# Two attentions on one core: B's memory update built as three-head bands in four 32-column quarters of the TensorE array, all five tiles in one PSUM bank

## The chip, the core and the metric

The kernel runs on one core of a Trainium2 chip. The core's engines run side by side, each through its own instruction stream in order: TensorE (PE, with its weight loads shown apart as PEld), VectorE (DVE), ScalarE (ACT), GpSimd (POOL) and SyncE (SP, which issues most transfers). They wait for one another through semaphores. The metric is the device time of one execution in microseconds, as the median of several runs; lower is better. A profile shows one execution, with the time of every instruction.

## What is computed

Two attention layers over 2048 positions with 32 heads of 18 columns each: A shares one key and value head among all query heads; B works in four segments of 512 positions and carries a memory from one segment to the next. The output is both results side by side. The change touches only the memory of B, whose part of the reference is this:

```python
phi = lambda t: jnp.where(t > 0, t + 1.0, jnp.exp(t))
for s in range(N):                       # N = 4 segments of L = 512
    qs, ks, vs = q[:, :, s], k[:, :, s], v[:, :, s]
    ...
    pq = phi(qs)
    num = jnp.einsum("bhld,bhde->bhle", pq, M)
    den = jnp.einsum("bhld,bhd->bhl", pq, z)[..., None] + 1e-6
    a_mem = num / den
    o = g * a_mem + (1.0 - g) * a_dot
    pk = phi(ks)
    M = M + jnp.einsum("bhld,bhle->bhde", pk, vs)    # per head 18 x 18
    z = z + jnp.einsum("bhld->bhd", pk)
```

## The kernel before

The program has two phases. The first (to line 606) makes the projections of A and then, in a loop over the four segments `s` of B, the projections of B, the stores of queries, keys and values to DRAM, and the memory. The second (from line 675) is the attention itself, whose order on PE, ACT and DVE is written out by hand; it begins after a branch on a flag that the first phase computes (line 609). The order of the first phase is set by a scheduler, from the order in which the code is written and its own costs; some instructions are pinned to program order (`pin`).

The 32 heads lie in five tiles of seven, seven, seven, seven and four heads (`HT`), so a tile has `RT` = 126 or 72 rows, 18 for each head; `H0` is a tile's first head. For each segment but the last, the keys after `phi` are transposed so that positions lie on partitions (`natural`, line 415, writes `pkN` with four blocks `i` of 128 positions). The values lie in `vch` in the same layout, with a column of ones ahead of each head's 18 values, so a head takes `VW` = 19 columns; the ones give `z`.

The update of the memory stands at the end of a segment's turn of the loop (lines 576 to 601). For each tile `t`, four matmuls over the four blocks of positions take all the tile's keys (126 columns of weights) times the values of all its heads (7 x 19 = 133 columns): a product of every key column with every head's values, of which only each head's own block is wanted. VectorE multiplies the product with a mask (`bmask`) that leaves the blocks on the diagonal, adds it into `Mbd`, copies the values' part to `Mst` and sums the column of ones into `zc` and from there into `zst`. The product of a tile goes to the PSUM tile `mm`, of which there is one buffer, so the next tile's matmuls wait until VectorE has read the one before. `Mst` and `zst` are the weights with which later queries read the memory: of segments 0 and 1 they are stored to DRAM (`mzB`, lines 600 and 601) and read back in the second phase, of segment 2 they are used in the first phase (lines 432 and 548).

Lines that the prediction names: 252 is a projection matmul (128 rows, 126 columns, 512 positions); 494 a projection of values; 418 a transposition of the keys after `phi`; 557 are the matmuls of the bound of the scores (32 columns of weights each, put side by side in the array); 582 the memory's matmuls; 591 to 598 its VectorE steps; 450, 122 and 391 what VectorE does with a projected key tile; 208, 214 and 216 the split of the next inputs on VectorE; 243 a split of weights on POOL; 381, 382 and 481 POOL's zeroing of `Mst`, `zst` and the ones of `vch`; 778 (output projection of the second phase) and 973 (probabilities times values) are the other matmuls of 32 columns of weights in four quarters.

An fp32 matmul shows in the profile as two records of PE (and two weight loads): line 582 has 5 x 4 matmuls in each of three segments and 120 records.

Of the kernel before, what the change touches and what calls it, by code (L numbers as in the profile page):

```python
# [8 lines left out]
F32 = mybir.dt.float32  # L9
# [5 lines left out]
ALU = mybir.AluOpType  # L15
AX = mybir.AxisListType
# [6 lines left out]
C = 512  # L23
NCH = S // C
NKT = S // 128
HT = [7, 7, 7, 7, 4]
RT = [18 * h for h in HT]
H0 = [0, 7, 14, 21, 28]
SCALE = DH ** -0.5
BOUND_UP = 1.0 + 2.0 ** -6  # L30

# [4 lines left out]
VW = DH + 1  # L36
# [38 lines left out]
def attention_pair_kernel(ctx, tc, a_xT, a_w, a_wo, b_xT, b_w, b_wo, b_beta, ident_d, hmask_d, bmask_d, cmask_d, sel_d, zmask_d, selx_d, sely_d, out):  # L75
    nc = tc.nc
# [79 lines left out]
    with ExitStack() as ph:  # L156
# [3 lines left out]
        ps = ph.enter_context(tc.tile_pool(name="ps", bufs=1, space=PSUM))  # L160
# [13 lines left out]
        bmask = pw.tile([128, 7, VW], F32, name="bmask")  # L174
        zmask = pw.tile([128, 5, 32], F32, name="zmask")
# [87 lines left out]
        for c in range(NCH):  # L263
            ready = {}
            if c == 0:
# [11 lines left out]
                for k in range(5):  # L277
# [3 lines left out]
                    for i, (w, x) in enumerate(parts_):  # L281
                        for t in TILES:
# [5 lines left out]
                                start=k == 0 and i == 0,  # L288
                                stop=k == 4 and i == 1,
# [8 lines left out]
            for t in TILES:  # L298
# [3 lines left out]
                else:  # L302

                    nm, bufs = ("nd", 2) if c == 1 and t == 4 else ("pj", 4)
                    pj = ps.tile([128, C], F32, name=nm, bufs=bufs)
                    proj(pj[:M], wAh, wAl, xh, xl, 126 * t, M)
                R = RT[t]
# [22 lines left out]
                i = 5 * (c - 2) + TILES.index(t)  # L330
# [31 lines left out]
        for t in range(5):  # L362
            R = RT[t]
# [11 lines left out]


        p2 = ph.enter_context(tc.tile_pool(name="p2", bufs=1))
        Mbd = p2.tile([128, 5, 7, VW], F32, name="Mbd")
        Mst = p2.tile([128, 5, 7, DH], F32, name="Mst")
        zst = p2.tile([128, 5, 32], F32, name="zst")  # L380
        nc.gpsimd.memset(Mst, 0.0)
        nc.gpsimd.memset(zst, 0.0)
        zc = p2.tile([128, 5], F32, name="zc")
# [21 lines left out]
        for s in range(NSEG):  # L405
# [6 lines left out]
            pkN = p2.tile([128, 5, 4, 126], F32, name="pkN")  # L412
# [67 lines left out]
            vch = p2.tile([128, 4, H, VW], F32, name="vch")  # L480
# [86 lines left out]
            with tc.issue_after(sent.ins):  # L567
# [5 lines left out]
                if s == 2:  # L573
                    load_q(st0, qA[0], 0)
                    load_shift(st0, shA[0], slice(0, 8))
            if s < NSEG - 1:
                for t in range(5):
                    R = RT[t]
                    nh = HT[t]
                    pm = ps.tile([128, C], F32, name="mm", bufs=1)  # L580
                    for i in range(4):
                        nc.tensor.matmul(
                            pm[:R, : nh * VW],
                            pkN[:, t, i, :R],
                            vch[:, i, H0[t] : H0[t] + nh, :].rearrange("p h d -> p (h d)"),
                            start=i == 0,
                            stop=i == 3,
                        )
                    pmv = pm[:R, : nh * VW].rearrange("p (h d) -> p h d", d=VW)
                    if s == 0:  # L590
                        nc.vector.tensor_tensor(Mbd[:R, t, :nh], pmv, bmask[:R, :nh], op=ALU.mult)
                    else:
                        mx = p2.tile([128, 7, VW], F32, name="mx", bufs=1)
                        nc.vector.tensor_tensor(mx[:R, :nh], pmv, bmask[:R, :nh], op=ALU.mult)
                        nc.vector.tensor_tensor(Mbd[:R, t, :nh], Mbd[:R, t, :nh], mx[:R, :nh], op=ALU.add)
                    nc.vector.tensor_copy(Mst[:R, t, :nh], Mbd[:R, t, :nh, 1:VW])
                    nc.vector.tensor_reduce(zc[:R, t : t + 1], Mbd[:R, t, :nh, 0], axis=AX.X, op=ALU.add)
                    nc.vector.tensor_scalar(zst[:R, t], zmask[:R, t], zc[:R, t : t + 1], None, op0=ALU.mult)
                if s + 1 in LATE_ASK:
                    nc.sync.dma_start(mzB[:, s, :, :126], Mst.rearrange("p t h d -> p t (h d)"))  # L600
                    nc.sync.dma_start(mzB[:, s, :, 126:], zst)
# [680 lines left out]
```

## Time and profile before

| what | value |
|---|---|
| median of three runs | 1412.04 us (1411.96 to 1413.07) |
| the profiled execution's own time | 1411.4 us |
| its span, first to last instruction | 1409.4 us |
| mean granted TensorE clock | 0.998 of full speed |
| PE busy | 1390.8 us, 99% of the span |
| DVE busy | 1047.8 us, 74% |
| ACT busy | 1198.2 us, 85% |
| first phase | from 0 to about 291 us |
| memory updates | 124.6 to 138.3 us, 177.8 to 191.1 us, 230.7 to 243.3 us |

Times are read from the start of the span. A row of the timeline gives the start, the time from the first start to the last end, the engine, line, operation, output and input, partitions x elements, and how many records were merged. PE's matmuls overlap: the time that a row of matmuls takes from the engine is the start of the next row less its own start, not its duration. A row of the windows gives the busy time of each engine in a stretch.

### The profile page before, as it was taken

To read this page: it belongs to the slowest core of one execution; us is meant where nothing else is said; L and a number is where in the kernel's file an instruction comes from. 1 tells how busy PE (TensorE), PEld (TensorE's weight loads), DVE (VectorE), ACT (ScalarE), POOL (GpSimd) and SP (SyncE) were. 2 spreads that over 40 slices of the span, in tenths; PEclk is the share of its full clock that TensorE was granted. 3 is DMA by queue.
4 is the path that set the end of the run, shared out by engine and by line. 5 is a ranking of instruction groups with operands and counts; after the bars stand their busy time and mean duration, and the time that the engine had idled before them with its cause. 6 is when DMAs were issued, how large, how long until landed. Compare 5 with 4: busy or idle time off the path is not lost.

```text
span 1409.4 us, 40568 instructions
## 1 busy us (share of the span) xinstructions
PE 1390.8 (99%) x17132; PEld 844.2 (60%) x17132; DVE 1047.8 (74%) x1567; ACT 1198.2 (85%) x1479; POOL 231.3 (16%) x326
## 2 busy tenths in 40 slices
PE   9999999989999999999999999999999999999998
PEld 6788888745544555555555555555555555555558
DVE  6656456477787778777878878776879778887873
ACT  4543434479999999999999999999999999999991
POOL 2431000003302310402110122113010220001002
PEclk9999999999999999999999999999999999999999
DMA  9866547467575445332312442333103321120012
GB/s 284 265 208 189 165 138 228 165 174 204 173 214 167 117 140 172 99 119 85 111 58 70 147 143 60 95 107 90 51 35 97 105 75 46 33 64 18 18 65 107
DMA packets 90724, 172.67 MB, mean 123 GB/s; under 512 B 14576, under 2 KB 22889, under 8 KB 90110
## 3 DMA queue, kind: packets, MB, share of 16 engines
q1 hardware_dynamic: 84122, 160.01, 36.7%
q0 software_dynamic: 1664, 4.78, 1.4%
q10 hardware_dynamic: 4752, 5.24, 1.1%
q8 instruction: 136, 2.23, 0.7%
q14 instruction: 50, 0.41, 0.1%
HBM read 99.32 MB, written 70.67 MB: 121 GB/s over the span
## 4 chain that ended last, share of the span: by engine, by line
PE 70%; ACT 4%; DVE 2%; issue 1%; DMA 1%; SPq 0%; POOL 0%; ACTq 0%; DVEq 0%
PE O L973 32%; PE E L925 20%; PE F L778 11%; ACT P L943 4%; PE E L933 3%; PE E L1183 2%; DVE W L940 1%; PE F L834 1%; DMA vseg<-vB 0%; DVE sm L729 0%; DMA woA<-a_wo 0%; PE F L1183 0%; PE O L1183 0%; DMA oA<-oe 0%; DVE oe L982 0%
## 5 line engine op out<-in xcount | busy, mean ns | idle before, releaser
L943 ACT ACTIVATE P<-E 128x1024 f32<-128x1024 f32 (+1 forms) x800 | 786.7, 1073 | 2.8 <-PE E L925 2.5
L940 DVE COPY W<-E 128x1024 f32<-128x1024 f32 (+2 forms) x416 | 453.8, 1091 | 142.4 <-PE E L925 81.2
L973 PE MATMUL O<-P,VA 128*32 128x256 f32 x7504 | 507.8, 380 | 0.0
L943 ACT ACTIVATE P<-W 128x1024 f32<-128x1024 f32 (+1 forms) x330 | 369.5, 1120 | 8.6 <-DVE W L940 7.9
L973 PEld LDWEIGHTS O<-P,VA 128*32 128x32 f32 x7504 | 259.7, 110 | 138.3 <-issue 6.2
L925 PE MATMUL E<-stA,kstA 56*128 56x512 f32 x1920 | 317.7, 430 | 3.9 <-DVE W L940 2.9
L925 PEld LDWEIGHTS E<-stA,kstA 56*128 56x128 f32 x1920 | 154.9, 185 | 161.4 <-issue 92.5
L948 POOL TENSOR_SCALAR_AFFINE_SELECT P<-P 128x256 f32<-128x256 f32 (+1 forms) x192 | 94.6, 493 | 416.9 <-ACT P L943 380.1
L762 POOL TENSOR_TENSOR o<-o,rb 126x512 f32<-126x512 f32 (+1 forms) x55 | 72.6, 1347 | 488.0 <-DVE PD L908 332.7
L778 PE MATMUL F<-woB,o 126*32 126x192 f32 (+1 forms) x1920 | 126.6, 338 | 0.0
L973 PE MATMUL O<-PD,VA 128*32 128x256 f32 x688 | 88.9, 379 | 0.0
L778 PEld LDWEIGHTS F<-woB,o 126*32 126x32 f32 (+1 forms) x1920 | 38.7, 108 | 74.6 <-issue 68.7
L973 PE MATMUL O<-P,vseg 128*32 128x256 f32 (+2 forms) x1536 | 81.5, 344 | 0.1
L901 DVE TENSOR_SCALAR PD<-E 128x512 uint32<-128x512 f32 x86 | 59.4, 691 | 26.6 <-PE E L925 25.1
L982 DVE COPY oe<-O 128x512 f32<-128x512 f32 x64 | 44.3, 692 | 41.4 <-PE O L973 40.5
L252 PE MATMUL pj<-xh,wBl 128*126 128x512 f32 x180 | 72.5, 404 | 0.0
L252 PE MATMUL pj<-xh,wBh 128*126 128x512 f32 x180 | 71.9, 400 | 0.0
L121 ACT CAST qp<-pj 126x512 fp32r<-126x512 f32 (+1 forms) x54 | 30.9, 584 | 45.0 <-DVE kmB L450 32.9
L778 PE MATMUL F<-woA,o 126*32 126x192 f32 (+1 forms) x960 | 63.9, 338 | 0.0
L122 DVE TENSOR_TENSOR qp<-pj,qp 126x512 fp32r<-126x512 f32 (+1 forms) x54 | 36.7, 685 | 36.2 <-ACT qp L121 36.0
L973 PEld LDWEIGHTS O<-P,vseg 128*32 128x32 f32 x1536 | 48.9, 110 | 24.4 <-issue 1.9
L933 PE MATMUL E<-stB 56*128 56x256 f32 (+3 forms) x512 | 61.4, 348 | 2.0 <-ACT P L943 1.3
(195 smaller groups left out, 1587.2 us busy)
## 6 DMA issues: line engine op xcount, KB each, us to landing
stB<-kB SPq DMA_DIRECT2D x96, 144.0 KB
stB<-qB SPq DMA_DIRECT2D x32, 288.0 KB
stA<-qA SPq DMA_DIRECT2D x30, 288.0 KB
oA<-oe SPq DMA_DIRECT2D x32, 256.0 KB
oB<-oe SPq DMA_DIRECT2D x32, 256.0 KB
qA<-qp SPq DMA_DIRECT2D x16, 504.0 KB
kB<-qp SPq DMA_DIRECT2D x16, 504.0 KB
qB<-qp SPq DMA_DIRECT2D x16, 504.0 KB
```

What stands on the lines that cost most here:

```text
L122: hold(nc.vector.tensor_tensor(qp[:R, 1, :n], src, qp[:R, 0, :n].bitcast(F32), op=ALU.subtract))
L252: nc.tensor.matmul(dst, w[:, c0 : c0 + M], x, start=i == 0, stop=i == len(ops) - 1)
L762: ins = tc.keep_in_program_order(nc.gpsimd.tensor_tensor(dst, a, b, op=op))
L778: nc.tensor.matmul(dst[32 * j : 32 * j + 32], parts[ab, c][: RT[t], t, r0 : r0 + 32], wo[ab][: RT[t], t, c0 : c0 + n], start=start, stop=stop,
L901: v.tensor_scalar(y, e, EXP_A, EXP_B, op0=ALU.mult, op1=ALU.add)
L925: nc.tensor.matmul(e[:, j], kstA[rows, 128 * kt : 128 * kt + 128], st[rows, h, :], start=True, stop=True)
L933: nc.tensor.matmul(e[:, j, c0 : c0 + 512 - 128 * k], st[rows, 4 + h, ks], st[rows, h, 128 * k :], start=True, stop=True)
L940: gate.append(nc.vector.tensor_copy(src[:, hs, :n], e[:, hs, :n]))
L943: nc.scalar.activation(p[:, hs, :n], src[:, hs, :n], AF.Exp, scale=SCALE)
L948: nc.gpsimd.affine_select(diag, diag, pattern=[[0, 2], [0, m], [1, 128]], base=0, channel_multiplier=-1, compare_op=ALU.is_ge, fill=0.0)
L973: nc.tensor.matmul(o[32 * j : 32 * j + 32, q0 : q0 + n], v, p[:, j % 2, p0 : p0 + n], start=m == hf == 0, stop=last and hf == 1,)
L982: nc.vector.tensor_copy(osb, o)
```

## The change

The update computes less and is spread otherwise. A tile's keys are cut at every 32 columns; a quarter touches at most three heads, whose values begin at `FIRST[...][g]`. For each quarter `g` a matmul multiplies its 32 (30 or 8 at a tile's end) key columns with the 57 columns of these three heads; the results of the quarters go to their own 32 partitions, side by side, and the five tiles lie side by side in the 285 columns of one PSUM tile. `Mbd` shrinks to three heads per row, `bands` is the mask cut in the same way, made once on POOL from `bmask`; `mx` gets a place of its own. VectorE then works on all tiles at once: two multiplications (tiles 0 to 3, tile 4), one addition, seven copies to `Mst` (for each quarter the three heads' places differ), one sum, and the five steps to `zst` as before.

```diff
+FIRST = [(0, 1, 3, 4), (0, 1, 1)]
...
-        Mbd = p2.tile([128, 5, 7, VW], F32, name="Mbd")
+        Mbd = p2.tile([128, 5, 3, VW], F32, name="Mbd")
+        mx = p2.tile([128, 5, 3, VW], F32, name="mx")
...
+        nc.gpsimd.memset(Mbd, 0.0)
+        nc.gpsimd.memset(mx, 0.0)
+        bands = p2.tile([128, 2, 3, VW], F32, name="bands")
+        for n, t in ((0, 0), (1, 4)):
+            for g, w in enumerate(FIRST[n]):
+                rows = slice(32 * g, min(32 * g + 32, RT[t]))
+                nc.gpsimd.tensor_copy(bands[rows, n], bmask[rows, w : w + 3])
...
             if s < NSEG - 1:
+                pm = ps.tile([128, C], F32, name="mm", bufs=1)[:, : 5 * 3 * VW].rearrange("p (t m) -> p t m", t=5)
                 for t in range(5):
-                    R = RT[t]
-                    nh = HT[t]
-                    pm = ps.tile([128, C], F32, name="mm", bufs=1)
                     for i in range(4):
-                        nc.tensor.matmul(
-                            pm[:R, : nh * VW],
-                            pkN[:, t, i, :R],
-                            vch[:, i, H0[t] : H0[t] + nh, :].rearrange("p h d -> p (h d)"),
-                            start=i == 0,
-                            stop=i == 3,
-                        )
-                    pmv = pm[:R, : nh * VW].rearrange("p (h d) -> p h d", d=VW)
-                    if s == 0:
-                        nc.vector.tensor_tensor(Mbd[:R, t, :nh], pmv, bmask[:R, :nh], op=ALU.mult)
-                    else:
-                        mx = p2.tile([128, 7, VW], F32, name="mx", bufs=1)
-                        nc.vector.tensor_tensor(mx[:R, :nh], pmv, bmask[:R, :nh], op=ALU.mult)
-                        nc.vector.tensor_tensor(Mbd[:R, t, :nh], Mbd[:R, t, :nh], mx[:R, :nh], op=ALU.add)
-                    nc.vector.tensor_copy(Mst[:R, t, :nh], Mbd[:R, t, :nh, 1:VW])
-                    nc.vector.tensor_reduce(zc[:R, t : t + 1], Mbd[:R, t, :nh, 0], axis=AX.X, op=ALU.add)
-                    nc.vector.tensor_scalar(zst[:R, t], zmask[:R, t], zc[:R, t : t + 1], None, op0=ALU.mult)
+                        for g in range(4 if t < 4 else 3):
+                            rows = slice(32 * g, min(32 * g + 32, RT[t]))
+                            h = H0[t] + FIRST[t == 4][g]
+                            nc.tensor.matmul(
+                                pm[rows, t],
+                                pkN[:, t, i, rows],
+                                vch[:, i, h : h + 3, :].rearrange("p h d -> p (h d)"),
+                                start=i == 0,
+                                stop=i == 3,
+                            )
+                new = mx if s else Mbd
+                for n, (R, ts) in enumerate(((126, slice(0, 4)), (72, slice(4, 5)))):
+                    nc.vector.tensor_tensor(
+                        new[:R, ts].rearrange("p t h d -> p t (h d)"),
+                        pm[:R, ts],
+                        bands[:R, n : n + 1].rearrange("p t h d -> p t (h d)").to_broadcast([R, ts.stop - ts.start, 3 * VW]),
+                        op=ALU.mult,
+                    )
+                if s:
+                    nc.vector.tensor_tensor(Mbd[:126], Mbd[:126], mx[:126], op=ALU.add)
+                for ts in (slice(0, 4), slice(4, 5)):
+                    for g in range(4 if ts.start < 4 else 3):
+                        rows = slice(32 * g, min(32 * g + 32, RT[ts.start]))
+                        w = FIRST[ts.start == 4][g]
+                        nc.vector.tensor_copy(Mst[rows, ts, w : w + 3], Mbd[rows, ts, :, 1:VW])
+                nc.vector.tensor_reduce(zc[:126], Mbd[:126, :, :, 0], axis=AX.X, op=ALU.add)
+                for t in range(5):
+                    nc.vector.tensor_scalar(zst[: RT[t], t], zmask[: RT[t], t], zc[: RT[t], t : t + 1], None, op0=ALU.mult)
                 if s + 1 in LATE_ASK:
                     nc.sync.dma_start(mzB[:, s, :, :126], Mst.rearrange("p t h d -> p t (h d)"))
```

The scheduler orders the first phase anew. On PE, at the end of segment 0, a row before was a matmul of line 582 with all of a tile's columns, and the tiles stood apart, with the next segment's projections (line 252) and a transposition (418) between them:

```order
L582 MATMUL mm<-vch,pkN 126x133 x4
L252 MATMUL pj<-xh,wBl 126x512
L252 MATMUL pj<-xh,wBh 126x512
L252 MATMUL pj<-xl,wBh 126x512
L582 MATMUL mm<-vch,pkN 126x133 x4
L252 MATMUL pj<-xh,wBl 126x512
L252 MATMUL pj<-xh,wBh 126x512
L252 MATMUL pj<-xh,wBl 126x512
L252 MATMUL pj<-xh,wBh 126x512
L582 MATMUL mm<-vch,pkN 126x133 x4
L252 MATMUL pj<-xl,wBh 126x512
L418 MATMUL tr<-ident,kf 128x126 x3
```

Now, on PE at the same place, the 76 matmuls of all five tiles (line 592 of the changed kernel, 16 for each of four tiles and 12 for the last) follow one another, broken only by the last two matmuls of the bound (line 566, which was 557); these rows are the beginning:

```order
L566 LDWEIGHTS kbB
L566 MATMUL nd<-aq,kbB 32x512
L592 MATMUL mm<-vch,pkN 32x57 x3
L592 MATMUL mm<-vch,pkN 30x57
L592 MATMUL mm<-vch,pkN 32x57 x3
L592 MATMUL mm<-vch,pkN 30x57
L592 MATMUL mm<-vch,pkN 32x57
L566 LDWEIGHTS kbB
L566 MATMUL nd<-aq,kbB 32x512
L566 LDWEIGHTS kbB
L566 MATMUL nd<-aq,kbB 32x512
L592 MATMUL mm<-vch,pkN 32x57 x2
```

What moved: nothing stands between the tiles any more, and the next segment's projections begin behind the whole update. On DVE, at the end of segment 0, the steps of the five tiles were spread among the work on the next segment's keys and inputs (450, 454, 122, 208):

```order
L134 TENSOR_TENSOR shp<-sht,shp 128x512
L591 TENSOR_TENSOR Mbd<-mm,bmask 126x133
L450 TENSOR_REDUCE kmB<-pj 126x1
L596 COPY Mst<-Mbd 126x126
L597 TENSOR_REDUCE zc<-Mbd 126x1
L454 TENSOR_SCALAR kbB<-zmask,kmB 126x32
L598 TENSOR_SCALAR zst<-zmask,zc 126x32
L208 CAST xh<-xr 128x512
L591 TENSOR_TENSOR Mbd<-mm,bmask 126x133
L122 TENSOR_TENSOR qp<-pj,qp 126x512
```

Now they stand together on DVE, with only one step of the next segment (line 459, which was 450) among them:

```order
L135 TENSOR_TENSOR shp<-sht,shp 128x512
L601 TENSOR_TENSOR Mbd<-mm,bands 126x228
L601 TENSOR_TENSOR Mbd<-mm,bands 72x57
L613 COPY Mst<-Mbd 32x4x54 x3
L613 COPY Mst<-Mbd 30x4x54
L613 COPY Mst<-Mbd 32x54 x2
L613 COPY Mst<-Mbd 8x54
L614 TENSOR_REDUCE zc<-Mbd 126x5
L459 TENSOR_REDUCE kmB<-pj 126x1
L616 TENSOR_SCALAR zst<-zmask,zc 126x32 x4
L616 TENSOR_SCALAR zst<-zmask,zc 72x32
L123 TENSOR_TENSOR qp<-pj,qp 126x512
```

What moved: the first step (line 601) now needs the last of the 76 matmuls, and the splits of the inputs (208, 214) come behind the update instead of between its tiles.

## The prediction

> **What bounds the kernel now.** The chain of waits that ended last reaches back in time only to the second phase (its first piece and PE's first matmul there are below), so for the stretch that the change touches I read the busy time of the engines in windows: the first phase cut at the three memory updates. Columns: the stretch, its length, then busy time and records of PE, PEld, DVE, ACT, POOL, the granted clock, the DMA share, GB/s.
>
> ```profile
> 290.62 0.17 issue
> ```
>
> ```profile
> 290.80 1.24 PE L925 MATMUL E<-st,kstA 56*128 56x512 f32 x6 [1.41 <-SPq L610]
> ```
>
> ```profile
> 78.00:124.00 46.00, 45.28 (x269) 38.52 (x262) 23.67 (x44) 19.72 (x42) 14.27 (x20) 1.00 0.61 181
> 124.00:137.00 13.00, 13.00 (x82) 10.46 (x81) 11.14 (x32) 3.19 (x7) 0.00 (x0) 1.00 0.74 243
> 137.00:177.00 40.00, 40.00 (x232) 35.19 (x232) 19.88 (x44) 18.41 (x40) 0.35 (x1) 1.00 0.55 166
> 177.00:190.00 13.00, 13.00 (x82) 10.62 (x81) 12.18 (x38) 4.56 (x8) 0.35 (x1) 1.00 0.67 225
> 245.00:290.00 45.00, 44.38 (x232) 34.02 (x230) 18.86 (x34) 16.10 (x35) 0.00 (x0) 1.00 0.52 178
> ```
>
> PE has no gap from 124 to 190 us. DVE is the only other engine near its limit, and only during the updates: 11.14 of 13.00 us and 12.18 of 13.00. So a microsecond of PE time saved in an update brings everything behind it forward by a microsecond, unless DVE then sets the pace. The second phase begins when the first has ended and runs by an order written out by hand that the change does not touch; it moves as a block.
>
> **What PE spends on the update now.** The timeline of PE at the end of segment 0 (start, duration, operation, count):
>
> ```profile
> 123.93 0.40 PE L252 MATMUL pj<-xh,wBl 128*126 128x512 f32 x1
> 124.26 0.40 PE L557 MATMUL nd<-aq,kbB 126*32 126x512 bf16 x3
> 124.59 0.72 PE L582 MATMUL mm<-vch,pkN 128*126 128x133 f32 x4
> 125.24 0.39 PE L557 MATMUL nd<-aq,kbB 126*32 126x512 bf16 x2
> 125.56 0.72 PE L582 MATMUL mm<-vch,pkN 128*126 128x133 f32 x4
> 126.03 0.47 PE L252 MATMUL pj<-xh,wBh 128*126 128x512 f32 x1
> 126.34 0.39 PE L252 MATMUL pj<-xl,wBh 128*126 128x512 f32 x1
> ...
> 131.20 1.07 PE L582 MATMUL mm<-vch,pkN 128*126 128x133 f32 x8
> 132.02 0.47 PE L252 MATMUL pj<-xh,wBl 128*126 128x512 f32 x1
> 132.33 0.39 PE L252 MATMUL pj<-xh,wBh 128*126 128x512 f32 x1
> 132.56 0.40 PE L252 MATMUL pj<-xl,wBh 128*126 128x512 f32 x1
> ```
>
> Read the starts. Eight records of one tile hold PE from 131.20 to 132.02, 0.82 us. The first projection behind them takes 0.31 us (132.02 to 132.33) where the next takes 0.23 (to 132.56): each return from the update costs 0.08 us, and five returns in a segment 0.4 us. Windows laid over the stretches of the update alone (the two L557 stretches within the first of them) end in these sums, one for each of the three segments:
>
> ```profile
> sum 4.94, PE 4.94 PEld 4.36 DVE 3.53 ACT 1.88 POOL 0.00; mean PE 0.99 PEld 0.87 DVE 0.71 ACT 0.38 POOL 0.00
> sum 4.72, PE 4.72 PEld 4.13 DVE 4.72 ACT 1.70 POOL 0.00; mean PE 0.94 PEld 0.83 DVE 0.94 ACT 0.34 POOL 0.00
> sum 4.70, PE 4.70 PEld 4.11 DVE 4.12 ACT 2.19 POOL 0.00; mean PE 0.94 PEld 0.82 DVE 0.82 ACT 0.44 POOL 0.00
> ```
>
> With the returns that is 5.34, 5.12 and 5.10 us: **15.56 us of PE** in all, of which the matmuls of L557 are part.
>
> **What PE will spend on it.** A segment now has 16 matmuls for each of four tiles and 12 for the last, 76, each two records: 152 records of 57 columns in place of 40 of 133 or 76. No such record exists before. The nearest are the other matmuls with 32 columns of weights, four quarters at a time, in the second phase:
>
> ```profile
> 1368.11 1.81 PE L778 MATMUL F<-woB,o 126*32 126x192 f32 x40
> 1369.74 0.40 PE L973 MATMUL O<-P,VA 128*32 128x256 f32 x4
> 327.89:328.00 0.11, 0.11 (x8) 0.11 (x4) 0.11 (x1) 0.11 (x2) 0.00 (x0) 1.00 0.53 149
> ```
>
> Forty records of 192 columns take 1.63 us (1368.11 to 1369.74), 41 ns each, though one alone lasts far longer: the quarters run side by side. The window of 0.11 us lies in a stretch of 128 columns: four weight loads (the x4 of PEld), a set of four records, 27 ns each. From 192 to 128 the time falls with the columns (41 x 128/192 = 27). So for 57 columns: if it keeps falling, 41 x 57/192 = 12 ns a record, 1.84 us a segment; if it stops at the narrowest that the trace shows, 152 x 27 = 4.1 us; if the longer burst holds PE to the 41 ns that it sustains at 192, 6.2 us. The full-width rows did fall with the columns (the eight records of 133 took 0.82 us, those of 76 below took 0.49), which speaks for the low end:
>
> ```profile
> 240.93 0.69 PE L582 MATMUL mm<-vch,pkN 128*72 128x76 f32 x8
> 241.42 0.48 PE L252 MATMUL pj<-xh,wBh 128*126 128x512 f32 x1
> ```
>
> Against it speaks the rate: 12 ns a record is over twice the fastest in the trace, and 304 weight loads and matmuls in a row are more than any burst there. Between 12 and 27 ns I take 21, a little nearer the row in the trace: **3.2 us a segment**.
>
> To that come the L557 stretches, which I keep at 0.33 (124.26 to 124.59) and 0.32 us (125.24 to 125.56), one return of 0.08, and 0.10 for the change from quarters to full width (L252 before L557 takes 0.33, 123.93 to 124.26, where the usual is 0.23): 0.83. A segment then costs 4.03 us, three 12.09: **3.5 us less**.
>
> A page of the Trainium skill speaks against the cut: TensorEngine Tiling (Array Packing), section Instruction Overhead, says that every matmul carries some 60 cycles of overhead, that one with a single column takes as long as one with 60, and that no tiling should be drawn from a dimension that is small already. At the 2.4 GHz of the same skill's TensorE: Matmul & The Clock Gate that is 25 ns, an estimate; if it holds for every record, 152 x 25 is 3.8 us in place of 3.2, and 1.7 us are saved in place of 3.5. The trace's 27 ns at 128 columns neither shows nor excludes it.
>
> **DVE.** The steps fall from 25 (20 in segment 0) to 16 (15), but they are larger:
>
> ```profile
> L594 DVE TENSOR_TENSOR mx<-mm,bmask 126x133 f32<-126x133 f32 x8 | 2.4, 294 | 0.9 <-PE mm L582 0.9
> L594 DVE TENSOR_TENSOR mx<-mm,bmask 72x76 f32<-72x76 f32 x2 | 0.5, 231 | 0.0
> L596 DVE COPY Mst<-Mbd 126x126 f32<-126x126 f32 x12 | 3.3, 277 | 0.1
> L597 DVE TENSOR_REDUCE zc<-Mbd 126x1 f32<-126x7 f32 x12 | 1.9, 155 | 0.0
> L598 DVE TENSOR_SCALAR zst<-zmask,zc 126x32 f32<-126x32 f32 x12 | 3.0, 253 | 0.1
> ```
>
> From 76 to 133 columns a multiplication grows by 63 ns, 1.1 ns a column: 228 columns cost 0.40, 57 columns 0.21, the addition of 285 about 0.46. The copies have 216 (four) and 54 columns (three); at 277 ns for 126 they cost at most 0.28 x 216/126 = 0.47, and at most 0.28: 2.7 together. One sum 0.16, five steps to `zst` 1.27. That is 5.2 us at most, against 4 x (294 + 292 + 277 + 155 + 253) ns plus about 1.0 for the last tile, 6.1, before (the addition taken like the multiplication). DVE loses no time and wins about 1 us in a place where it is nearly full; I count that as nothing, since PE has no gap there that it could close.
>
> The new wait: line 601 needs the last of the 76 matmuls. In segment 0 DVE comes to it at 130.5, when it started the first multiplication before:
>
> ```profile
> 129.91 0.69 DVE L134 TENSOR_TENSOR shp<-sht,shp 128x512 fp32r<-128x512 f32 x1
> 130.52 0.29 DVE L591 TENSOR_TENSOR Mbd<-mm,bmask 126x133 f32<-126x133 f32 x1
> ...
> 138.08 0.23 DVE L598 TENSOR_SCALAR zst<-zmask,zc 72x32 f32<-72x32 f32 x1
> ```
>
> PE is through the block at 124.26 + 4.0 = 128.3, so 2 us cover the wait. In segments 1 and 2 the cover is about nothing, and DVE may wait up to a microsecond with 134, 214 and 450 queued behind it; PE has four buffers for projected tiles (14 records of 0.23 us each, 3.2 us a tile) before it would feel that. Nothing counted.
>
> **POOL and SP.** Two memsets of 285 columns, seven small copies; they stand ahead of these:
>
> ```profile
> 79.28 0.62 POOL L381 MEMSET Mst<- 128x630 f32 x1 [2.67 <-PE nd L365]
> 80.01 0.35 POOL L481 MEMSET vch<- 128x128 f32 x1
> 85.62 1.27 POOL L243 TENSOR_TENSOR wBl<-wr,wBh 128x504 fp32r<-128x504 f32 x1 [5.27 <-ACT wBh L242]
> ```
>
> At 0.35 us or less each they take about 3 us, inside the 5.27 that POOL then waits for ACT. Without that cover they would put the split of weights back by 3 us. SP's two stores of the memory move ahead of a key store and an input load; before, the last step to `zst` started at 138.08, now it should by about 130.5 + 5.2 = 135.7, so SP is not held longer. Nothing counted.
>
> **The sum.** The page's first line:
>
> ```profile
> span 1409.4 us, 40568 instructions
> ```
>
> Span 1409.4 - 3.5 = 1405.9; the profiled execution took 1411.4, two more than its span, which gives 1407.9; the median shown is 0.6 above that execution: **1408.5 us**.
>
> **The rivals.**
> *A, full shrinking* (12 ns a record): 3 x (1.84 + 0.83) = 8.0, 7.5 us saved, 1404.5. For it, 192 to 128 and 133 to 76 columns; against it, the rate that no burst shows.
> *B, a floor at the narrow row* (27 ns): 3 x 4.93 = 14.8, 0.8 saved, 1411.3, no change that can be told. The page above is this mechanism in another form.
> *C, the long burst is slower* (41 ns, at the block of 76 matmuls): 3 x 7.03 = 21.1, 5.5 lost, 1417.5. It decides once a record costs over 29 ns (15.56 = 3 x (0.83 + 152 x 29 ns)). For it: all sustained bursts of the trace stay at 41 ns or more; against it: those are explained by their columns.
> *D, DVE sets the pace* (full in 12.18 of 13.00): PE finishes early and waits for a buffer; the saving is given back, 1412. Against it, DVE's own load falls.
> *E, the quarters don't run side by side*: each record costs alone what 76 columns do, 61 x 57/76 = 46 ns, 7.0 us a segment, 3 x 7.83 = 23.5, 7.9 lost, 1419.9. The L778 and L973 rows speak against it.
>
> **Chances.** A difference under 0.2% (2.8 us) can't be told from no change here. The forecast's case (15 to 25 ns) 0.34, of it 0.26 faster and 0.08 the same; A 0.20, faster; B 0.14, the same; C 0.20, slower; D 0.07, of it 0.05 the same, 0.02 slower; E 0.05, slower. Faster 0.46, the same 0.27, slower 0.27. The range reaches down to A's 1404.0 and up towards C, leaving out E and C's upper half: 1404.0 to 1416.0; the forecast's case alone holds 1405.5 to 1410.5.
>
> **What would show it.** In the profile after, the records of line 592, 456 of them, should start at a mean of 21 ns apart within a segment, the block (bound and memory) should last about 4.0 us from the first row of the bound, and the second phase should begin at about 287 in place of 290.8 us. PE must stay without gaps from 124 to 190; a wait of PE for DVE behind the block would show D. A mean of 12, 27 or 41 ns shows A, B or C. The forecast is wrong if the second phase itself changes its length by more than a microsecond, or if the update is not where the difference lies.

## The result, and the profile after

The changed kernel took **1408.89 us** (median of 8 runs, 1408.09 to 1409.47), the kernel before, run beside it, 1412.86 (8 runs, 1411.96 to 1414.34): a ratio of 0.9972, 95% interval 0.9962 to 0.9981. It is 0.28% faster. The profiled execution of it took 1409.3 us, with a span of 1407.5 us, 1.9 less than before; the account below is of these two profiled executions, and some 2 us more between the medians are not in it.

The time almost equals the forecast, but its parts do not. Lines shift by 9 or 10 in the first phase and 18 in the second: 557 is now 566, 582 is 592, 418 is 427, 391 is 400, 450 is 459, 925 is 943. First the timeline of PE at the end of segment 0, which answers to the one in the prediction (start, duration, operation, count, idle time before it):

```profile
124.33 0.39 PE L253 MATMUL pj<-xh,wBl 128*126 128x512 f32 x1
124.65 0.40 PE L566 MATMUL nd<-aq,kbB 126*32 126x512 bf16 x3
124.68 0.66 PE L592 MATMUL mm<-vch,pkN 128*30 128x57 f32 x18
125.40 0.39 PE L566 MATMUL nd<-aq,kbB 126*32 126x512 bf16 x2
125.41 2.09 PE L592 MATMUL mm<-vch,pkN 128*32 128x57 f32 x134
127.43 0.50 PE L253 MATMUL pj<-xh,wBh 128*126 128x512 f32 x1
...
137.80 0.62 PE L427 MATMUL tr<-ident,kf 126*128 126x126 f32 x4 [1.77 <-DVE kf L400]
```

The block runs from 124.65 to 127.43, 2.78 us for bound and memory together. Read its row of 134 records: 2.02 us, 15.1 ns each; inside the block the starts of the single records come in sets of four (of three in the last tile), every 50 ns, **12.5 ns a record** in a full set. The rows of L592 begin 0.03 us after the first row of L566: the bound's matmuls take quarters too, and the two are interleaved. That saves little: where a run below moves the update away from the bound, its 152 records alone hold PE for 2.13 us (14.0 ns each) and the bound alone for 0.64, together the same 2.77. Only the third block, 2.55 us, is some 0.2 shorter. And ten microseconds later PE stands still for 1.77 us, where it had no gap before. Windows over the three blocks, then over the time from the first block to the second phase, and the second phase (stretch, length, busy time and records of PE, PEld, DVE, ACT, POOL, granted clock, DMA share, GB/s):

```profile
124.65:127.43 2.78, 2.71 (x158) 2.42 (x157) 1.60 (x4) 1.18 (x3) 0.00 (x0) 1.00 0.75 251
177.47:180.25 2.78, 2.71 (x158) 2.42 (x157) 2.78 (x6) 1.87 (x4) 0.00 (x0) 1.00 0.65 225
229.47:232.02 2.55, 2.55 (x159) 2.40 (x158) 2.01 (x5) 1.66 (x4) 0.00 (x0) 1.00 0.71 233
...
124.65:287.73 163.08, 158.63 (x1276) 131.33 (x1276) 89.65 (x199) 63.91 (x134) 1.05 (x3) 1.00 0.58 185
...
287.73:1407.50 1119.77, 1106.01 (x15600) 610.43 (x15600) 880.66 (x1215) 1077.77 (x1239) 186.91 (x266) 0.99 0.34 101
```

The same two stretches of the kernel before:

```profile
124.26:290.80 166.54, 165.13 (x941) 137.44 (x940) 92.73 (x222) 64.19 (x134) 1.05 (x3) 1.00 0.56 181
...
290.80:1409.40 1118.60, 1104.42 (x15600) 611.00 (x15600) 880.42 (x1215) 1077.16 (x1239) 186.48 (x266) 1.00 0.33 101
```

This is the account of the change. From the first block on, PE's busy time fell by 6.50 us (165.13 to 158.63), but its idle time rose from 1.41 to 4.45 us, so the second phase came 3.46 us sooner after the block. The second phase then took 1.17 us longer. With 0.39 us lost before the first block (124.26 to 124.65, ahead of everything that the change touches on PE and DVE) the span fell by 1.9. Where the idle time went, in the view of waits of PE from 120 to 300 us (who waited for whom, us, times, longest):

```profile
PE tr L427 <- DVE kf L400: 2.7, 2, 1.8
PE E L943 <- SPq L628: 1.6, 1, 1.6
PE E L943 <- issue: 1.0, 1, 1.0
```

Before, the wait at this place was:

```profile
PE tr L418 <- DVE kf L391: 0.2, 1, 0.2
```

So there are two questions: why PE waits for `kf`, and why the second phase grew. DVE's timeline, first two rows of before, then the changed kernel, shows what stands ahead of `kf`:

```profile
130.94 0.69 DVE L450 TENSOR_REDUCE kmB<-pj 126x1 f32<-126x512 f32 x1
...
135.10 0.68 DVE L391 SCALAR_TENSOR_TENSOR kf<-pj,ph_e 126x512 f32<-126x512 f32 x1
```

```profile
130.69 0.51 DVE L601 TENSOR_TENSOR Mbd<-mm,bands 126x228 f32<-126x228 f32 x2
131.54 1.74 DVE L613 COPY Mst<-Mbd 32x216 f32<-32x216 f32 x7 [0.34 <-DVE Mbd L601]
133.31 0.18 DVE L614 TENSOR_REDUCE zc<-Mbd 126x5 f32<-126x15 f32 x1
133.41 0.68 DVE L459 TENSOR_REDUCE kmB<-pj 126x1 f32<-126x512 f32 x1
134.00 0.81 DVE L616 TENSOR_SCALAR zst<-zmask,zc 126x32 f32<-126x32 f32 x5
...
136.98 0.68 DVE L400 SCALAR_TENSOR_TENSOR kf<-pj,ph_e 126x512 f32<-126x512 f32 x1
```

The key maximum `kmB` (line 459) started at 130.94 before and now starts at 133.41, behind the update's steps; ACT's cast of the same tile begins 0.07 us after it ends, and `kf` follows at 136.98 (135.10 before). And PE has less to do meanwhile: four of the five pieces of the update used to run behind the next segment's first projections, and now all of it runs ahead of them.

### The profile page after: what moved, and what is told of

It is laid out like the page before. It is cut to its first block, busy times and chain, and to the rows that moved or that the text cites. A ratio compares the mean times of both kernels' runs of the same rounds, so it can differ in the third digit from the quotient of the medians.

```text
span 1407.5 us, 41225 instructions
## 1 busy us (share of the span) xinstructions
PE 1386.2 (98%) x17468; PEld 837.5 (60%) x17468; DVE 1045.7 (74%) x1544; ACT 1198.8 (85%) x1479; POOL 234.4 (17%) x335
## 4 chain that ended last, share of the span: by engine, by line
PE 71%; ACT 4%; DVE 2%; issue 1%; DMA 1%; POOL 0%; SPq 0%; ACTq 0%
PE O L991 33%; PE E L943 21%; PE F L796 11%; ACT P L961 4%; PE E L951 3%; PE E L1201 2%; DVE W L958 1%; PE F L852 1%; DMA vseg<-vB 0%; DMA woA<-a_wo 0%; DVE sm L747 0%; PE F L1201 0%; PE O L1201 0%; DVE o L857 0%; DVE oe L1000 0%
```

## The experiments

Each was profiled once and timed beside the kernel before. Since executions differ in their first 100 us, the stretch from the first block to the second phase, and the second phase itself, are compared within one profile.

**Taking the DVE steps away, and the whole update.** In the first run the steps behind the matmuls are handed out in the next segment, in the second they are left out, in the third the matmuls too.

```diff
-                new = mx if s else Mbd
...
+                todo.append((s, pm))
...
+                if t == 4:
+                    finish_update()
```

> The DVE steps of the update (multiplication by the bands, addition, copies to Mst, the sum, zst, and the two stores) are handed out in the next segment, behind its fifth key tile; the matmuls stay where they are. Theory (DVE holds PE back): after the change PE waits 1.77 and 0.97 us for the copy of kf, because the update's DVE steps stand in one block ahead of the key maximum kmB, on which the casts, ph_e and kf follow. With the block gone from there the two waits fall below 0.5 us in total, the second phase's first matmul starts about 2.3 us earlier than the 287.73 of the changed kernel (about 285.4), and the median falls by 1 to 3 us, to 1406 to 1408. Rival (kf is late for the splits of the next input piece, or for ACT, and not for the update): the waits stay at 2 us or more, the second phase starts at 287 to 288, and the median stays within 0.7 us of 1408.9.

Measured 1410.09 us, ratio 0.9979 (0.9969 to 0.9988): no faster than the changed kernel. The start of `kmB` (7.8 us behind the block's first row, 8.8 in the changed kernel) and the first wait did move, but the sum did not. The waits of PE:

```profile
PE tr L454 <- DVE kf L400: 1.2, 2, 1.0
...
PE tr L454 <- DVE kbB L490: 0.8, 1, 0.8
PE tr L454 <- DVE zst L424: 0.8, 1, 0.8
```

2.8 us, as in the changed kernel. The first wait fell from 1.77 to 0.83 us, but the moved steps make a new one of 0.8 where they stand now (`zst`), and the one of segment 1 stayed at about 1. The theory is half right for segment 0 and wrong for the whole.

> The changed kernel without any DVE step of the update (the stores of the memory stay, and send zeros): what is left out is the banding, the sum over segments, Mst and zst, so the answer to the memory's part is missing. Theory (DVE holds PE back): as with the late DVE steps, the waits of PE for kf go, the second phase starts at about 285, and the median is 1405.5 to 1408. Rival: what was given back after the change hangs on PE itself (the switch from quarters to full width, the returns), and the start stays at 287 to 288.

Measured 1413.13 us, ratio 1.0003 (0.9995 to 1.0012), not faster than the kernel before, with less work. The waits at the transposition of `kf` are 1.8 and 1.4 us, with no DVE step of the update left. DVE's timeline shows the next in line:

```profile
135.72 0.43 DVE L209 CAST xh<-xr 128x512 fp32r<-128x512 f32 x1 [1.07 <-DMA xr<-b_xT]
136.07 0.68 DVE L459 TENSOR_REDUCE kmB<-pj 126x1 f32<-126x512 f32 x1
```

The scheduler now has the split of an input piece ahead of `kmB`, and that waits 1.07 us for its load. So the theory falls: the update's DVE steps are one of several things that can stand ahead of `kmB`. The run also lost 2.1 us earlier in segment 0, since the order changed there too, so its total is no price of the DVE steps.

> The changed kernel without the update at all: its matmuls and DVE steps are left out, the stores of the memory stay and send zeros. Theory: a set of four quarter records costs PE 50 ns, 152 records 1.9 us a segment, so beside the kernel without DVE steps the second phase starts 5.7 us earlier, at about 279.5, and the span falls by as much less a microsecond or so at the start of the second phase: median 1400 to 1403. This is the most that any form of the update could win. Rival (the first phase is held by DVE or by the loads once PE is faster): less than 3 us earlier than without the DVE steps.

Measured 1404.91 us, ratio 0.9942 (0.9929 to 0.9955). From the first row of the bound to the second phase it takes 154.69 us, 8.39 less than in the changed kernel, and PE waits for `kf` nowhere. PE is busy for 6.44 us less there and idle for 1.95 less: the update's rows, three times 2.13 us, and the waits for `kf`, 2.74 us, are gone, and a wait of 0.7 us for the bound is new. The median still misses the expected 1400 to 1403. The order ahead of the bound changed too, so that it comes at 131.32: from the values to it PE stood idle for 3.44 us, where it had 0.16 in the changed kernel, and ran at half clock for 3.41. So the 4 us between 1408.89 and 1404.91 are no bound on what another form of the update could still win.

**The price of a record.** First each tile's matmuls twice over:

```diff
-                    for i in range(4):
+                    for i in (0, 1, 2, 3, 0, 1, 2, 3):
```

> Each tile's quarter matmuls are issued twice over, the second pass overwriting the first: 304 records in a segment in place of 152, the result is the same. Theory (a steady 12.5 ns a record, and DVE late in any case): 1.9 us more in each block, 5.7 in all, of which the waits for kf, 2.75 us, take up about 2.5: the second phase starts at 290 to 292, the median is 1411 to 1413.5. Rival 1 (nothing waits behind the block, each microsecond of PE counts): 293.4, 1414.6. Rival 2 (a longer burst comes to the 41 ns that the 192-column records sustain): blocks of over 8 us, 1420 or more.

Measured 1424.41 us, ratio 1.0085 (1.0071 to 1.0099), 15.5 us over the changed kernel. The time is that of the second rival, 1420 or more, but not its mechanism: the records keep their price, and PE pauses. The profiled execution was the fastest of six, 1419.6 us. The timeline of PE in its three blocks:

```profile
124.60 3.40 PE L592 MATMUL mm<-vch,pkN 128*32 128x57 f32 x240
129.33 0.99 PE L592 MATMUL mm<-vch,pkN 128*32 128x57 f32 x46 [1.33 <-issue]
...
186.12 1.80 PE L592 MATMUL mm<-vch,pkN 128*30 128x57 f32 x113 [1.85 <-issue]
...
244.77 1.06 PE L592 MATMUL mm<-vch,pkN 128*32 128x57 f32 x52 [3.09 <-issue]
```

The blocks last 6.40, 6.88 and 8.14 us. Without the pauses that is 5.07, 5.03 and 5.05, some 2.3 us or 15 ns a record for the 152 more, near the 14.0 ns of the first. But in the middle of each burst PE stands still for 1.3 to 3.1 us, and the profile names only issue. Instructions come in pieces of 16 KB on the profile's q8, which I take for PE's own by the count: in the changed kernel 17,468 matmuls and as many weight loads in 138 pieces are 253 to a piece. At 12.5 ns a record such a piece lasts 1.6 us. In each block the pause ends 2.3 to 2.5 us after a piece begins to come (127.02, 183.76, 242.31).

Then one head's values in each quarter, 19 columns, with VectorE's multiplication cut to match:

```diff
-                                pm[rows, t],
+                                pm[rows, t, :VW],
...
-                                vch[:, i, h : h + 3, :].rearrange("p h d -> p (h d)"),
+                                vch[:, i, h],
```

> The changed kernel with one head's values in each quarter in place of three: 19 columns in a matmul in place of 57, as many matmuls and weight loads; two thirds of the memory are left out. It prices a record. Theory 1 (the time falls with the columns): a set of four quarter records comes every 17 to 20 ns in place of 50, the block of segment 0 takes about 1.5 us in place of 2.79. Theory 2 (a record can't be issued faster than some floor, the weight loads or the 25 ns per matmul of the Trainium skill): a set stays at 50 ns if the weight loads set it, or comes every 25 ns if 25 ns hold within a quarter, or every 100 ns if they held for all records together (which the 50 ns at 57 columns already exclude).

Measured 1405.42 us, ratio 0.9948 (0.9933 to 0.9964). The sets of four come every 30 to 37 ns, some 8 ns a record, and the block with the bound takes 2.13 us: between the theories. A third of the columns takes two thirds of the time, so part of a record's time does not fall with the columns. The two waits for `kf` are 1.2 us here, with the block in its old place but 0.65 us shorter and its first VectorE step smaller.

**The place of the block.** The update, matmuls included, behind the second key tile's projection; then the bound with it:

```diff
+                if t == 1:
+                    update()
+                    pkN = None if last else p2.tile([128, 5, 4, 126], F32, name="pkN")
                 if t and not last:
                     natural(f, pkN[:, t - 1, :, 0:126], 0, 126)
```

> The changed update, matmuls and DVE steps alike, is handed out in the next segment, behind the projection of its second key tile, so that PE meets the block after 28 projections and not before them; nothing is left out. Theory A (place of the block): kf of the first key tile is late because the block of 2.8 us stands on PE ahead of that tile's projection, and then no update is left to fill PE's time until kf is there; before the change four of the five pieces stood behind that projection. Behind it, the block covers the wait: PE's two waits for kf, 2.75 us in the changed kernel, fall below 0.8 us, and from the first row of the bound in segment 0 to the first matmul of the second phase it takes 160.0 to 161.2 us (163.08 in the changed kernel, 166.54 before); the median falls by about 2 us to 1406 to 1407.5. Theory B (kf is late for what stands ahead of it on DVE, the splits of the next input piece among it, wherever the block is): the waits stay at 2 us or more and the stretch at 162.5 to 163.5 us.

Measured 1408.28 us, ratio 0.9969 (0.9958 to 0.9980). The waits at the transposition, of PE:

```profile
PE tr L466 <- DVE kf L400: 0.8, 2, 0.4
PE tr L466 <- DVE kbB L505: 0.4, 1, 0.4
```

1.2 us in place of 2.74, though not the expected 0.8. The place of the block does matter, but not it alone: the run with one head's values comes to 1.2 us too. Yet the stretch gains only 0.53:

```profile
124.31:286.86 162.55, 159.78 (x1277) 130.51 (x1276) 89.75 (x199) 64.00 (x134) 1.07 (x3) 1.00 0.58 185
```

PE's idle time fell by 1.68 us (4.45 to 2.77), its busy time rose by 1.15. The reason is in the timeline of the bound and of the update, which now stand apart:

```profile
124.31 0.40 PE L608 MATMUL nd<-aq,kbB 126*32 126x512 bf16 x3
124.63 0.50 PE L253 MATMUL pj<-xh,wBh 128*126 128x512 f32 x1
124.97 0.39 PE L253 MATMUL pj<-xl,wBh 128*126 128x512 f32 x1
125.29 0.39 PE L608 MATMUL nd<-aq,kbB 126*32 126x512 bf16 x2
125.61 0.50 PE L253 MATMUL pj<-xh,wBl 128*126 128x512 f32 x1
...
131.82 2.21 PE L413 MATMUL mm<-vch,pkN 128*32 128x57 f32 x152
133.95 0.50 PE L253 MATMUL pj<-xh,wBh 128*126 128x512 f32 x1
```

The bound holds PE twice for 0.32 us, the update for 2.13 (131.82 to 133.95). A projection before or behind such a row takes 0.32 to 0.34 us in place of 0.23: 0.1 us each way, 0.2 for there and back. Three ways there and back in a segment in place of one, in three segments, are 1.2 us, about the rise.

> Both the bound of a segment (its five matmuls and the steps behind them) and the update are handed out in the next segment, behind the projection of the second key tile, so that PE runs them as one block there. Measured from PE's first row of the values in segment 0 to the first matmul of the second phase (195.86 us before the change, 192.40 after it, 191.88 with the update alone moved). Theory: each return from the quarters to the full width costs PE some 0.2 us, and the update alone moved had three such in a segment, this has one; the waits for kf stay at 1.2 us or less: 190.9 to 191.6 us. Rival (the bound's four steps on DVE now stand ahead of kf): the waits rise to 2 us or more, 192.2 us or more. Median 1407 to 1408.5 by the theory, 1409 or more by the rival.

Measured 1415.58 us, ratio 1.0019 (1.0010 to 1.0028): slower than before. From the values to the second phase it takes 199.65 us, far over the 192.2 from which the rival counted. The waits at the transposition rise to 4.3 us, as the rival had it, and one block of 152 records now pauses like those of 304:

```profile
239.84 2.28 PE L429 MATMUL mm<-vch,pkN 128*32 128x57 f32 x146
245.08 0.29 PE L429 MATMUL mm<-vch,pkN 128*32 128x57 f32 x6 [2.96 <-issue]
```

**The second phase.** Its first rows on PE in the changed kernel, which answer to the 290.80 row of before:

```profile
287.73 1.12 PE L943 MATMUL E<-st,kstA 56*128 56x512 f32 x4 [1.57 <-SPq L628]
289.81 1.65 PE L943 MATMUL E<-st,kstA 56*128 56x512 f32 x6 [0.96 <-issue]
```

After four matmuls PE pauses for 0.96 us; a piece of its instructions began to come at 287.40, 2.4 us before the end of the pause. The next run moves all of the second phase's instructions by 128 places without running any:

```diff
                 store_max(mc, shX, h)
+                pm = pgs.tile([128, 4, 512], F32, name="gps")
+                for _ in range(64):
+                    nc.tensor.matmul(pm[:, 0, :128], qs[:KP, :128], ks[:KP, :128], start=True, stop=True)
```

> The changed kernel with 64 more matmuls inside the branch that is not taken between the two phases: nothing more runs, but PE's instructions of the second phase lie 128 places later. Theory (instruction transfer): the stall of 0.96 us after the first matmuls of the second phase, for which the profile names only issue, is PE waiting for its next 16 KB of instructions, whose transfer begins at 287.40 as the second phase starts; where the phase begins inside such a piece decides. Moved by 128 instructions the stall goes (or moves to a place where PE has no work for it), the second phase falls from 1119.8 us to 1118 to 1119.2, and the median by 0.5 to 1.5 us. Rival (the stall belongs to the branch, or to ACT): it stays, and the median stays within 0.5 us of 1408.9.

Measured 1411.13 us, ratio 0.9987 (0.9978 to 0.9996), 2.2 us over the changed kernel. PE:

```profile
292.00 1.95 PE L946 MATMUL E<-st,kstA 56*128 56x512 f32 x6 [4.45 <-DMA vB<-vch]
294.21 2.16 PE L946 MATMUL E<-st,kstA 56*128 56x512 f32 x6 [0.26 <-ACT P L964]
```

The position decides, but with the other sign: the pause is gone, and the gap ahead of the phase grew from 1.57 to 4.45 us. A piece begins to come at 289.19, 2.8 us before the phase's first matmul; I infer that no instruction behind the branch was in hand when it was taken. (The releaser named is the last store of values; in the changed kernel the phase began at 287.73, before that store's packets moved at about 288.3, so it is not the cause.)

> Both of the two edits before: the update behind the second key tile's projection, and 64 matmuls in the branch not taken. If theory A of the place and the theory of the instruction transfer hold, both gains add: median 1405 to 1406.5. If neither holds it stays at 1408 to 1409.5.

Measured 1411.10 us, ratio 0.9989 (0.9980 to 0.9998), with a gap of 4.35 us: the same loss on top of the other edit, so a second time the unexecuted matmuls alone cost 2 to 3 us.

If the edge of a piece is what counts, 128 instructions that do run move it past the branch:

```diff
+                if s == 0:
+                    for m in range(32):
+                        rows = slice(32 * (m % 4), min(32 * (m % 4) + 32, 126))
+                        nc.tensor.matmul(bank[rows, 400:401], pkN[:, 0, 0, rows], vch[:, 0, 0, 0:1], start=True, stop=True)
```

> The changed kernel with 32 one-column matmuls behind the block of segment 0, in a corner of the bank that nobody reads: 64 records and 64 weight loads more, 128 instructions of PE that run ahead of the second phase at under 0.5 us. Refined theory of the instruction transfer: PE holds two pieces of 16 KB, 256 instructions each; in the changed kernel only some 10 of those behind the branch are in hand when it is taken, and 64 matmuls not run (128 places) put them all out of hand (a gap of 4.45 in place of 1.57 us). 128 places that are run move the edge of the pieces past the branch: 10 - 128 + 256, about 138 are in hand. So no stall of issue after the first matmuls, a gap ahead of the second phase of at most 1.8 us, and the second phase 0.5 to 1.2 us shorter than 1119.8 where the half clock lasts as long; median 1407.5 to 1408.9. Rival (no such pieces): the stall of about 1 us or the gap of over 4 us is there again, median 1409 or more.

Measured 1408.70 us, ratio 0.9974 (0.9965 to 0.9983). PE at the start of the second phase, and the phase as a window:

```profile
288.16 1.51 PE L948 MATMUL E<-st,kstA 56*128 56x512 f32 x6 [1.51 <-SPq L633]
290.08 2.02 PE L948 MATMUL E<-st,kstA 56*128 56x512 f32 x6 [0.40 <-ACT P L966]
```

```profile
288.16:1405.40 1117.24, 1104.82 (x15600) 610.00 (x15600) 880.54 (x1215) 1076.94 (x1239) 186.35 (x266) 1.00 0.33 101
```

No pause, no long gap: in these the theory holds. The phase of 1117.24 us in place of 1119.77 is 2.5 shorter, more than the 0.5 to 1.2 expected. The small matmuls lengthen the block of segment 0 by 0.5 us, and from the values to the second phase it takes 192.96 us against 192.39. The profile's span is 2.1 us shorter than the changed kernel's, but this was the fastest of eleven executions; the medians cannot be told apart.

> The edits of the two runs before together: the block with the bound behind the second key tile, and 32 one-column matmuls in segment 0. If both theories hold the gains add, with the second phase's start free of a stall: median 1406 to 1407.8. If the shift does nothing it is as with the block alone.

Measured 1411.29 us, ratio 0.9989 (0.9979 to 0.9998). The pauses of the run with bound and update moved are gone, block and second phase alike, but for a new one of 0.4 us, and it gains 4.3 us over it; the waits at the transposition stay, and it is 2.4 us behind the changed kernel. The theory of the block with the bound falls here too.

**What the runs point to.** The update behind the projection in segments 0 and 1 alone, and the 32 small matmuls:

```diff
+            if s == NSEG - 2:
+                update()
```

> What the runs before point to: the update of segments 0 and 1 behind the second key tile's projection (where PE waited for kf), that of segment 2 in its place (where it waited for nothing), and 32 one-column matmuls behind the block of segment 0, which move the second phase's instructions past the edge of a piece. From PE's first row of the values in segment 0 to the first matmul of the second phase: 191.88 us with all three moved, less 0.5 for the switches that segment 2 is spared, plus 0.3 for the small matmuls where they outlast the wait for kf: 191.2 to 192.2 us (192.40 in the changed kernel). Second phase without a stall of issue, 1117.2 to 1118.6 us (1119.8 in the changed kernel). Median 1406.3 to 1408.3, under both kernels. If the place of the block gains nothing and the shift nothing: 1408.7 or more.

Measured **1408.22 us**, ratio 0.9969 (0.9957 to 0.9982). The second phase takes 1118.38 us without a pause of issue; the stretch from the values is 192.26 us against the changed kernel's 192.39, 0.06 outside the expected range. The median is the lowest of the versions that compute everything, but its interval covers the changed kernel's 0.9972: it beats the kernel before, and cannot be told from the changed one.

## Why the prediction came out right, point by point

*What bounds.* Right: no engine took PE's place for long, and a microsecond of PE's time counted until PE met a wait. (A detail: the range's lower end is called A's 1404.0, while A's sum gives 1404.5.)

*The price of a record: mis-sized.* 21 ns was taken as the mean of a block; a block standing alone measured 14.0 (152 records in 2.13 us, not 3.2), and 12.5 within a full set. In three segments the difference is 3.2 us. Rival A, full shrinking, had nearly the rate, and its time of 1404.5 did not come. The page weighed there, TensorEngine Tiling (Array Packing) of the Trainium skill, section Instruction Overhead, with its 60 cycles for each matmul, 25 ns by the prediction's estimate, did not bind as a price of every record: across the four quarters records follow at half of that, and at 8 ns with 19 columns. Within one quarter the runs don't contradict it: there they follow every 50 ns, and every 30 to 37 with 19 columns.

*The bound's stretches, kept at 0.65 us: right in two segments.* Blocks of 2.78, 2.78 and 2.55 us less the 2.13 of the memory leave 0.65, 0.65 and 0.42. With 0.1 us for the return, that is 8.4 in all against 15.56, 7.1 us less in place of 3.5; of the 3.7 us between 8.4 and the forecast's 12.09, 3.2 are the price of a record.

*DVE and its waits, "nothing counted": wrong.* PE was to feel a late DVE only when four buffers ran out. It met it at the transposition of `kf`, 1.77 and 0.97 us. That is rival D, a saving given back, at a place it didn't name. The runs show that neither DVE's steps alone nor the place of the block alone is the cause: without the first, the wait is 3.2 us; with the block elsewhere, 1.2, and as much with a shorter block in the old place. With no update at all there is none. What share each has stays open.

*The second phase "moves as a block": wrong by 1.17 us*, over the microsecond that the prediction gave itself, so by its own sign the forecast fails here. The pause of 0.96 us for instructions goes with it: six profiles with a pause of 0.96 to 1.7 us behind the first matmuls, the changed kernel's among them, have second phases of 1119.4 to 1120.1 us, the eight without one 1117.3 to 1119.1. What the clock adds, below, is not shown.

*The sum.* 3.5 us saved, as forecast, was 6.5 us of PE work less 3.0 of new idle time in the first phase, and the second phase took 1.2 of that back in the profiled execution. The medians differ by 4.0. So the number came out by luck: the saving on PE was nearly twice the forecast, and waits and a second phase that were counted as nothing took back the rest.

*SP and POOL, nothing:* no wait of PE in the profile after goes to either before the second phase; POOL's new steps (busy for 17.16 us from 78 to 124, 14.27 before) held PE up nowhere. The 0.39 us ahead of the first block stay open; in experiments that change nothing ahead of it the same point lay between 123.84 and 126.54 us.

## What to carry to other kernels

Packing the small matmuls into the quarters of the array and leaving out what nobody needs cut PE's time on update and bound from 15.6 to 8.4 us here; the bound, which ran on quarters already, kept nearly its price. Each way from the full width to the quarters and back cost 0.2 us here, so put such work side by side. Work that looks like pure cost may be the filler behind which a chain on other engines is hidden: before gathering it into one block, look for what PE will do while that chain runs. A change in the number of instructions can move another phase by 1 to 3 us, so compare phases, not only totals, before a difference of that size is put down to an idea.

## What the hardware showed that was not expected

**PE can outrun its instructions.** Bursts at 160 instructions a microsecond (12.5 ns for a matmul and its weight load) paused for 1.3 to 3.1 us, each pause ending 2.3 to 2.5 us after a 16 KB piece began to come; a block of 152 records passed without a pause in the changed kernel and paused for 2.96 us in another order. At the branch between the phases the place of the code decided between gaps of 1.5 and 4.4 us. That the place of the code decides is shown by moving it; that PE waits for the transfer itself rests on the times of the pieces, and how many pieces PE holds is not shown.

**The clock after the branch.** Windows at the start of the second phase, of the changed kernel and of the one before:

```profile
285.41:288.82 3.41, 1.84 (x10) 1.02 (x9) 0.00 (x0) 0.58 (x2) 0.00 (x0) 0.98 0.30 99
288.82:299.06 10.24, 8.38 (x48) 3.73 (x46) 7.28 (x11) 8.65 (x10) 0.22 (x1) 0.51 0.51 119
```

```profile
291.80:295.22 3.42, 1.65 (x10) 0.76 (x8) 3.22 (x6) 3.42 (x5) 0.44 (x1) 1.00 0.10 19
295.22:298.63 3.41, 3.41 (x26) 1.56 (x28) 3.34 (x5) 3.41 (x5) 0.00 (x0) 0.50 0.75 165
```

PE ran at half clock for 10.24 us in the changed kernel and for 3.41 before, 6.8 us longer; other runs had 6.83. These are one, two and three times 3.41, and the Trainium skill, TensorE: Matmul & The Clock Gate, Part 1, has a window of that length that runs freely and lowers the clock after an idle one: the trace agrees in length, but the stretches ahead were not idle: PE was busy for 1.84 and 1.65 us of their 3.41. What the longer stretch costs was not measured by itself, and its length does not sort the second phases: before the change 3.41 us at half clock went with 1118.60 us, 6.83 with 1117.24 in the run with the small matmuls, and 10.24 with 1119.09 in the run without the update.
